# Holding the filter once in 32-row blocks and summing the complex product ahead of the inverse transform, in a fused FFT mixing and maxout kernel

## The chip, the cores and the metric

One core of a Trainium2 chip. The metric is the device time of one execution in microseconds, the median of the runs. Engines: TensorE (PE) multiplies matrices, VectorE (DVE), ScalarE (ACT) and GpSimd (POOL) work on elements, SyncE (SP) issues DMAs. [...]

## The reference

For x of 8 x 3072 x 256 (float32), a filter F = filt_r + i filt_i of 1537 x 256, and weights w1, w2 (256 x 1024) and w_out (1024 x 256):

```python
X = np.fft.rfft(x, axis=1)
Y = X * F
y = np.fft.irfft(Y, n=3072, axis=1)      # 24576 rows of 256 after a reshape
out = np.maximum(y @ w1, y @ w2) @ w_out
```

## The kernel before

**The maths.** 3072 = 96 x 32. S1 is a transform over 96 points, S2 one over 32 points with the twiddle factors (table `U`, 24 blocks u of 64 columns: 32 real, 32 imaginary parts), then comes the product with F, then S3, the inverse of S2 (tables `VP` for the part multiplied by filt_r, `VQ` for that by filt_i), and S4, the inverse over 96. From batch 2 on S1 works on sums and differences of the two halves of the input, which POOL makes (`fold`, lines 103 and 104) from float32 tiles `XF` that SP loads. Between the stages a batch goes through DRAM (`ad` between S1 and S2, `zd` between S3 and S4), which turns its axes. Maxout is computed as max(y(w1-w2), 0) w_out + y w2 w_out: `Wd` = w1-w2, `M` = w2 w_out, so each tile of 384 rows needs 8 pairs of `ph` matmuls (`moe_h`, line 454, then a relu on ACT or DVE) and 30 `po` matmuls (`moe_o`, lines 484 and 486).

**The filter.** `F` (line 51) has 128 partitions: for each of two groups g the rows 64g to 64g+31 hold the filter (16 rows of k, 16 of the mirrored 96-k), and rows 64g+32 to 64g+63 the same again, since S2 puts real parts in the first 32 rows and imaginary parts in the next 32. `load_f` loads one copy with 16 POOL DMAs, `double_f` makes the second: for h = 0 four DVE copies, for h = 1 four DMAs on SP. `put_fz` and `fix_f` put in the rows for k = 0, 48 and 1536.

**A visit.** The transforms of the next batches are threaded through the maxout of this one. The loop at line 709 runs 64 steps a batch: `moe_h` of one block, then a visit if one is planned for this step, then 3 or 4 `moe_o` matmuls, then the other planned work (`todo`: loads, folds, reads), then, once in 8 steps, `s4`. A visit n (line 415) does S3 of visit n-1 (line 405, 16 matmuls of 64x64 tiles), S2 of two of the 12 w (line 381, 8 matmuls), S1 of some quads of the next batch (line 354, 4 matmuls each) and the products of this S2 (line 387). A product is one DVE operation over 128 x 1024 that reads a PSUM tile `px` and writes px times filt_r and px times filt_i in bf16; S3 then adds real and imaginary parts in PSUM, by a second matmul with `VQ`. There are 7 visits to a batch, planned by hand in `plan_f2` (line 682), as are the loads (`xs`), the folds and the reads.

**PSUM.** The pool `ps` has six banks for everything but the outputs, which have two of their own (`pso`). A new tile takes the bank that was released first and waits until what was in it has been read.

**Order.** The program has `manual_schedule`: every engine and every DMA queue executes its instructions in the order of the program. What stands behind a waiting instruction waits too.

**The opening** handles batch 0 on its own path: `s1t`, transposes `t1`, S2, products shared by DVE and POOL (`products`, line 608; POOL's take a copy `xs` in SBUF that ACT makes, line 603), `s3t`, transposes `t2`, `s4`. The tables VP and VQ are made from U in `table_v` and `put_v`. POOL's queue there is: loads of x, loads of F, products, then the load of batch 1's quads 4 to 7 of 16 (line 645), Wo, Wd (lines 646 to 648), the rest of batch 1, and w2.

## Time and profile before

| | us |
|---|---|
| median of 3 runs | 501.41 (500.83 to 502.92) |
| span of the profiled execution, first to last instruction | 499.6 |
| median less that span | 1.8 |
| PE busy, span 62 to 490 | 427.65 of 428.00 |
| PE busy, span 0 to 36 | 27.15 of 36.00 |
| DVE, ACT, POOL busy over the span | 329.9, 309.0, 258.7 |

A line of the timeline reads: start and duration in us, engine, line of the kernel, operation, out<-in by the program's names, shape, count; in brackets how long the engine was idle ahead of it and what ended that. For PE the shape has the tile of the array (64*64) ahead of the operand's. A group of the profile reads: the same names, count | busy us, mean ns of one | idle time ahead and what ended it. The profiled execution has no time of its own beside its span; the runs were other executions.

### The profile page before, as it was taken

What the parts mean: (1) busy time and instruction counts of PE and PEld (TensorE: products, weight loads), DVE (VectorE), ACT (ScalarE), POOL (GpSimd) and SP (SyncE); (2) the same over time, 40 slices, a digit from 0 to 9 for tenths busy, and PEclk for the clock granted to TensorE, in tenths of its full rate; (3) what the DMA queues carried; (4) which work ended last, traced back from release to release, by engine and by line L of the source; (5) the groups of instructions that cost most, each with busy time, mean ns of one, the idle gap of its engine ahead of it and who ended that gap; (6) DMA issues with size and microseconds to landing.
All of it is one profiled execution on the core that took longest, in us unless ns stands there. A gap on an engine that the chain in (4) does not pass through costs nothing.

```text
span 499.6 us, 13073 instructions
## 1 busy us (share of the span) xinstructions
PE 486.2 (97%) x5297; PEld 361.0 (72%) x5300; DVE 329.9 (66%) x515; ACT 309.0 (62%) x630; POOL 258.7 (52%) x342
## 2 busy tenths in 40 slices
PE   7689999999999999999999999999999999999996
PEld 3457767777777777777777777777777777777775
DVE  7786788458865578457865678557774588555552
ACT  5777478647774577646775577646676456544442
POOL 8795569637546584539547394438642221222220
PEclk9989999999999999999999999999999999999999
DMA  8989799997689768896489776896677625521112
GB/s 130 159 236 219 216 245 298 277 258 210 206 241 245 206 202 219 257 261 195 150 252 251 197 231 189 261 261 181 199 205 206 158 85 149 172 83 64 64 64 85
DMA packets 78046, 97.23 MB, mean 195 GB/s; under 512 B 8065, under 2 KB 54434, under 8 KB 77954
## 3 DMA queue, kind: packets, MB, share of 16 engines
q1 hardware_dynamic: 64786, 66.80, 50.5%
q0 software_dynamic: 13200, 29.60, 20.7%
q8 instruction: 41, 0.67, 0.6%
q14 instruction: 19, 0.16, 0.1%
HBM read 53.87 MB, written 47.19 MB: 202 GB/s over the span
## 4 chain that ended last, share of the span: by engine, by line
PE 83%; DMA 11%; POOL 3%; SPq 1%; DVE 1%; issue 1%; ACT 0%; POOLq 0%
PE po L486 32%; PE ph L454 30%; PE po L484 8%; PE pz L405 4%; PE py L434 4%; DMA zd<-zt 2%; DMA bt<-ad 2%; DMA WS<-in_moe_w_dram 2%; PE px L381 2%; PE pa L354 2%; DMA xb<-in_x_dram 2%; POOL F L121 1%; DMA ad<-at 1%; POOL xb L88 1%; DMA F<-in_filt_i_dram 1%; DMA zr<-zd 1%
## 5 line engine op out<-in xcount | busy, mean ns | idle before, releaser
L486 PE MATMUL po<-Wo,gt 128*128 128x256 bf16 x1536 | 261.1, 273 | 0.0
L458 ACT ACTIVATE gt<-ph 128x384 bf16<-128x384 f32 x321 | 157.6, 495 | 146.8 <-PE ph L454 145.7
L486 PEld LDWEIGHTS <-gt 128*128 128x128 bf16 x1536 | 146.0, 98 | 66.7 <-issue 12.0
L467 POOL DMA_DIRECT2D out_dram<-ot x186 | 102.7, 557 | 170.8 <-DVE ot L499 166.4
L456 DVE TENSOR_SCALAR gt<-ph 128x384 bf16<-128x384 f32 x191 | 104.5, 553 | 64.3 <-PE ph L454 60.7
L387 DVE TENSOR_TENSOR pq<-px,F 128x1024 bf16<-128x1024 f32 x91 | 106.9, 1219 | 26.4 <-PE px L381 26.2
L454 PEld LDWEIGHTS <-Wd 128*128 128x128 bf16 x1024 | 96.5, 98 | 12.2 <-issue 0.3
L103 POOL TENSOR_TENSOR xb<-XF 128x512 bf16<-128x512 f32 x48 | 61.2, 1275 | 52.8 <-DMA XF<-in_x_dram 52.0
L499 DVE COPY ot<-po 128x512 f32<-128x512 f32 x95 | 65.2, 686 | 24.9 <-PE po L486 24.8
L104 POOL TENSOR_TENSOR xb<-XF 128x512 bf16<-128x512 f32 x48 | 60.9, 1269 | 0.0
L358 ACT ACTIVATE at<-pa 128x512 bf16<-128x512 f32 x96 | 51.8, 612 | 4.6 <-PE pa L354 4.6
L409 ACT ACTIVATE zt<-pz 128x512 bf16<-128x512 f32 x84 | 45.6, 595 | 4.9 <-PE pz L405 0.8
L434 PE MATMUL py<-G,zr 96*128 96x96 bf16 x512 | 32.6, 206 | 0.1
L434 PEld LDWEIGHTS <-zr 96*128 96x128 bf16 x512 | 28.9, 97 | 2.4 <-DVE zr L563 0.6
L405 PE MATMUL pz<-pq,VP 64*64 64x256 bf16 x336 | 22.0, 281 | 0.0
L381 PE MATMUL px<-bt,U 64*64 64x256 bf16 x384 | 20.2, 278 | 1.3 <-ACT VQ L278 0.7
L405 PE MATMUL pz<-pq,VQ 64*64 64x256 bf16 x336 | 21.0, 269 | 0.0
L405 PEld LDWEIGHTS <-VP 64*64 64x64 bf16 x336 | 9.9, 105 | 13.3 <-issue 13.0
L354 PE MATMUL pa<-xb,CT 64*64 64x512 bf16 x192 | 18.1, 377 | 0.3 <-DVE y__1495 L440 0.3
L381 PEld LDWEIGHTS <-U 64*64 64x64 bf16 x384 | 10.5, 108 | 4.2 <-issue 3.6
L570 PE MATMUL pd<-W 128*128 128x512 bf16 x28 | 10.1, 474 | 1.5 <-DVE zero L149 1.5
L405 PEld LDWEIGHTS <-VQ 64*64 64x64 bf16 x336 | 10.0, 106 | 0.0
(428 smaller groups left out, 602.9 us busy)
## 6 DMA issues: line engine op xcount, KB each, us to landing
out_dram<-ot POOLq DMA_DIRECT2D x186, 128.0 KB, 3.7
XF<-in_x_dram SPq DMA_DIRECT2D x96, 192.0 KB, 4.6
ad<-at SPq DMA_DIRECT2D x56, 192.0 KB, 3.7
zd<-zt SPq DMA_DIRECT2D x42, 256.0 KB, 3.1
zr<-zd SPq DMA_DIRECT2D x56, 192.0 KB, 4.6
bt<-ad SPq DMA_DIRECT2D x13, 768.0 KB, 10.5
WS<-in_moe_w_dram SPq DMA_DIRECT2D x4, 512.0 KB, 8.1
xb<-in_x_dram POOLq DMA_DIRECT2D x8, 192.0 KB, 6.6
```

Of the source, the lines that this page charges most:

```text
L103: G.tensor_tensor(t_[:, 0], f[:, 0], f[:, 1], OP.add)
L104: G.tensor_tensor(t_[:, 1], f[:, 0], f[:, 1], OP.subtract)
L358: S.activation(at[:, m0:m0 + 2], pa[g], AF.Copy)
L387: E.tensor_tensor(pq, px.rearrange("p (o i) d -> p o i d", o=1).to_broadcast([128, 2, 2, D]), F[:, :, 2 * v:2 * v + 2, s], OP.mult)
L405: TE.matmul(pz[g][64 * s:64 * s + 64, i], tab[64 * g:64 * g + 64, 2 * v + i, s], pq[s][64 * g:64 * g + 64, q, i], start=(q == 0), stop=(q ...
L434: TE.matmul(py[:, m], zr[b][:, 4 * i + m, 128 * dc:128 * dc + 128], G1, start=True, stop=True)
L454: TE.matmul(ph, Wd[:, dc, 128 * j:128 * j + 128], y_[:, dc], start=(dc == 0), stop=(dc == 1))
L456: V.tensor_scalar(gt[tt][:, j], ph, 0.0, None, OP.max)
L458: S.activation(gt[tt][:, j], ph, AF.Relu)
L467: E.dma_start(out=dst, in_=ot[tt // 2][:, 3 * (tt % 2) + c])
L486: TE.matmul(p_, g_[:, n - 2, blk], Wo[:, n - 2], start=(e == 0), stop=(e == 9))
L499: V.tensor_copy(ot[tt // 2][:, e - 1:e + 1], po[q // 2 % 2])
```

## The change

The filter is held once, in blocks of 32 rows: partition 32q + r of `F` holds, for 6 values of j, the row for block u = 4j + q, so that all 128 partitions differ. S2 writes the real parts and the imaginary parts of four blocks side by side, as two column groups c of one PSUM tile. This takes 64x32 tiles (16 matmuls for what 8 did), and so does S1 (8 for 4). A product now multiplies both c by both parts of the filter, in float32, and the complex sum is made ahead of S3: real parts by a subtraction on DVE, imaginary parts by an addition on POOL, each 128 x 512. S3 then needs no second pass over `VQ`: it works in 32x64 tiles on four blocks of 32 rows, once for two j, three times a batch, with 32 matmuls each and four PSUM banks. The visits at steps 11, 16, 21, 27, 32, 37 and 47 do S3 at the fourth, sixth and seventh, and S1 in pairs of quads at the others; folds and loads are planned anew. In the opening no filter rows are doubled, `load_f` has 20 DMAs, the loads of w1 and w2 are held until POOL has issued them (`hold_w`), S3 takes four terms into one sum (`TERMS`), and the load of batch 1's quads 4 to 7 stands behind Wd.

```diff
-    def s2(b, v):
+    def s2(b, j):
         px = [ps.tile([128, 2, D], FP32, tag="ps", name="px%d" % s) for s in range(2)]
+        for c in range(2):
+            for q, s in ((0, 0), (1, 1), (2, 0), (3, 1), (0, 1), (1, 0), (2, 1), (3, 0)):
+                u = 4 * j + q
+                TE.matmul(px[s][32 * q:32 * q + 32, c], U[64 * s:64 * s + 64, u, 32 * c:32 * c + 32],
+                          bt[b][64 * s:64 * s + 64, u], start=True, stop=True)
+        return px
...
+    def products(b, j, px):
+        pq = pqpool.tile([128, 2, 2, 2, D], FP32, tag="pq", name="pq")
+        for s in range(2):
+            product(V, j, s, px[s], pq[:, s])
+        zc[b, j] = zcpool.tile([128, 2, 2, D], BF16, tag="zc", name="zc")
+        V.tensor_tensor(zc[b, j][:, :, 0], pq[:, :, 0, 0], pq[:, :, 1, 1], OP.subtract)
+        G.tensor_tensor(zc[b, j][:, :, 1], pq[:, :, 0, 1], pq[:, :, 1, 0], OP.add)
+
+    def s3(b, t):
...
+        pz = [ps.tile([128, 2, D], FP32, tag="ps", name="pz%d" % q) for q in range(4)]
         for i in range(2):
+            z_ = zc.pop((b, 2 * t + i))
+            for c in range(2):
+                for q, s in ((0, 0), (1, 1), (2, 0), (3, 1), (0, 1), (1, 0), (2, 1), (3, 0)):
+                    TE.matmul(pz[q][64 * s:64 * s + 64, i], VT[32 * q:32 * q + 32, c, 2 * t + i, s],
+                              z_[32 * q:32 * q + 32, s, c], start=(c == 0), stop=(c == 1))
...
+    def visit(b, ts, js, quads):
+        for t in ts:
+            s3(b, t)
+        pxs_ = [s2(b, j) for j in js]
         if b + 1 < B:
             for c in quads:
                 s1(b + 1, c)
+        for j, px in zip(js, pxs_):
+            products(b, j, px)
...
-        for g, r in ((0, 0), (1, 1), (0, 1), (1, 0)):
-            TE.matmul(pa[g][64 * r:64 * r + 64], CT[64 * g:64 * g + 64, r], xb[b, c][64 * g:64 * g + 64, r],
-                      start=True, stop=True)
+        for h in range(2):
+            for g, s in ((0, 0), (1, 1), (0, 1), (1, 0)):
+                TE.matmul(pa[g][64 * s + 32 * h:64 * s + 32 * h + 32], CT[64 * g:64 * g + 64, s, h],
+                          xb[b, c][64 * g:64 * g + 64, s], start=True, stop=True)
...
+    hold_w()
+    for h in range(2):
+        load_w(h)
...
+    pz = s3t(0)
+    for q in range(4):
+        put_z(0, q, S, pz)
+    pxs[4] = s2(0, 4)
+    stage_x(4, 1)
+    dve(4, 0)
+    pool_(4, 1)
...
-    load_x(1, 2, 2)
     load_wo()
     for q in range(4):
         prep_wd(q, G)
+    load_x(1, 2, 2)
     for c in (4, 6):
         load_x(1, c, 2)
...
+            ts = {3: (0,), 5: (1,), 6: (2,)}.get(n, ())
+            js = (n,) if n < 6 else ()
+            mid.setdefault((b, st), []).append((visit, (b + 1, ts, js, quads[n])))
...
+    plan_f2(0, (23, 27, 31, 35, 38, 42, 48), ((0,), (1,), (2, 3), (), (4, 5), (), ()),
+            (8, 10, 15, 18, 21, 27, 30, 33), (16, 19, 25, 28, 31, 34, 38, 42), 57)
+    mid[0, 45] = [(visit, (1, (), (), (6,)))]
+    mid[0, 51] = [(visit, (1, (), (), (7,)))]
+    plan_f2(1, (11, 16, 21, 27, 32, 37, 47), ((0, 1), (2, 3), (4,), (), (5, 6), (), (7,)),
+            range(-25, 31, 7), range(-15, 41, 7), 52)
+    for b in range(2, B - 1):
+        plan_f2(b, (11, 16, 21, 27, 32, 37, 47), ((0, 1), (2, 3), (4, 5), (), (6, 7), (), ()),
+                range(-32, 24, 7), range(-21, 35, 7), 38)
```

## The prediction

> **What bounds the kernel now.** First the busy rows. TensorE (PE) is busy for 97% of the span, and nothing else comes above 72%. Windows of the trace split that: PE misses 0.35 us of the 428.0 from 62 to 490, so time is won or lost there only by PE's own slots or by making PE wait. Before 36 us it misses 8.85, and there other chains decide.

> ```profile
> PE 486.2 (97%) x5297; PEld 361.0 (72%) x5300; DVE 329.9 (66%) x515; ACT 309.0 (62%) x630; POOL 258.7 (52%) x342
> ```

> Then PE's timeline around one visit (start, duration, line; a row's duration has the drain in it, so I count from start to start):

> ```profile
> 230.77 0.49 PE L454 MATMUL ph<-y__4292,Wd 128*128 128x384 bf16 x2
> 231.19 0.30 PE L405 MATMUL pz<-pq,VP 64*64 64x256 bf16 x4
> 231.32 0.28 PE L405 MATMUL pz<-pq,VQ 64*64 64x256 bf16 x4
> 231.43 0.28 PE L405 MATMUL pz<-pq,VP 64*64 64x256 bf16 x4
> 231.54 0.28 PE L405 MATMUL pz<-pq,VQ 64*64 64x256 bf16 x4
> 231.65 0.39 PE L381 MATMUL px<-bt,U 64*64 64x256 bf16 x8
> 231.87 0.39 PE L354 MATMUL pa<-xb,CT 64*64 64x512 bf16 x4
> 232.19 0.39 PE L486 MATMUL po<-Wo,gt 128*128 128x256 bf16 x2
> ```

> Four 64x64 tiles run side by side, and a set of four with 256 columns costs 0.109 us. S3 of one visit is 0.46, S2 0.22, S1 0.21. Entering tiled work costs 0.09 (two ph matmuls take 0.33, the visit begins 0.42 after them), leaving it 0.1 (0.32 for S1). Almost every visit looks like this, so hardly any waits for a bank now.

> Third, the engines that PE would wait for:

> ```profile
> L387 DVE TENSOR_TENSOR pq<-px,F 128x1024 bf16<-128x1024 f32 x91 | 106.9, 1219 | 26.4 <-PE px L381 26.2
> L103 POOL TENSOR_TENSOR xb<-XF 128x512 bf16<-128x512 f32 x48 | 61.2, 1275 | 52.8 <-DMA XF<-in_x_dram 52.0
> L104 POOL TENSOR_TENSOR xb<-XF 128x512 bf16<-128x512 f32 x48 | 60.9, 1269 | 0.0
> ```

> Last, the opening: POOL's timeline, and the row of PE's that takes the second half of batch 1's input.

> ```profile
> 33.55 0.56 POOL L88 DMA_DIRECT2D xb<-in_x_dram  x1
> 34.10 0.93 POOL L293 DMA_DIRECT2D Wo<-in_moe_w_out_dram  x1
> 35.02 2.52 POOL L297 TENSOR_TENSOR Wd<-WS 128x512 bf16<-128x512 f32 x2
> 37.71 2.50 POOL L297 TENSOR_TENSOR Wd<-WS 128x512 bf16<-128x512 f32 x2 [0.17 <-DMA WS<-in_moe_w_dram]
> ```

> ```profile
> 40.97 0.38 PE L329 MATMUL pa<-xb,C 96*96 96x512 bf16 x1
> ```

> **The change, part by part.** The sum is made against the span, 499.6; the median of the runs is 501.4, 1.8 more, and that is added at the end.

> *S3.* A batch had 6 x 16 matmuls in fours; it has 3 x 32 in eights. No row shows 32x64 tiles. The best end is eight in the time of four: 3 x 0.46 instead of 6 x 0.46, -1.38 a batch, -9.7 over seven batches. The worst is no overlap beyond four, 0. The nearest rows are 64x32 tiles (lines 266 and 268): with 64 columns eight begin in about 0.033 us, against 0.031 for four 64x64 ones at line 264. That is overlap by eight, so I take -9.7.

> *S1 and S2* have twice the matmuls of half the width, by the same rows in the same time: 0. [...]

> *Tilings.* S3 and S2 no longer share one. Two visits of a batch change it midway, at an entry's 0.1: +0.2 a batch, with batch 1's extra stretch +1.6.

> *Banks.* PSUM pool `ps` has six, and every visit follows a ph. A ph's bank comes free 0.85 (ACT) or 0.92 us (DVE) after its second matmul begins, 0.60 to 0.67 into the visit, and some 0.05 later PE knows. A visit with S2 and two S1 quads takes six banks and wants the sixth at 0.22+0.21 = 0.43: a wait of 0.23. (Today's six-bank visits want it at 0.68 or later, so they don't wait.) There are 21 such visits; six hide it under the next item's wait: 15 x 0.23 = +3.4. S3 with S2 wants its sixth at 0.56: 14 x 0.13 = +1.8. Two stalls of today, 0.65 at 69 us and 0.37 at 113, go. Sum +4.2.

> *POOL's sum in front of the folds.* This is the dearest item. Today POOL has nothing of the products. After, each visit puts a 128x512 sum on POOL that waits for both of DVE's products, and POOL keeps its order, so a fold planned just behind a visit waits too. For batches 1 to 5 the last fold stands at step 27 or 28, right behind the visit at 27, and its S1 at step 32. From the first S3 matmul of visit 27: S2's second set begins at 0.46+0.1+0.11 with 0.13 for the bank, 0.80; DVE starts 0.32 after it (231.76 to 232.08); two products take 2.27 (232.08 to the next DVE start, 234.35): 3.4; POOL's sum, as line 103, 1.27: 4.7; the fold 2.5: 7.2. PE gets there by 0.46+0.1+0.22+0.1+0.13 for visit 27, 4.02 for five steps (0.33 a ph pair, 0.109 an output matmul, 0.34 for s4, 0.09 to enter) and 0.43 of S2 and the first S1: 5.5. It waits 1.7, five times: +8.5. In batch 0 the sums of steps 23 and 27 and the folds of 25 and 28 stand in one row on POOL; fold 3 ends 6.7 after visit 27 begins, S1 wants it at 4.3: +2.3. The other quads, worked out alike, have one us to spare or more. Sum +10.8.

> *DVE's subtraction* (128x512, two SBUF inputs) has no row of its size. Below it is 0.38 (line 233, 192 elements), above 0.96 (line 244, 768); between them 0.70 as a duration and, by the 0.1 that DVE's rows overlap, 0.6 from start to start. A visit then takes 2.87 of DVE instead of 2.27. A five-step stretch with its visit lasts 4.02+0.76 = 4.8; DVE's other work is 2.76 in eight steps (three relus and a y of 0.465, 1.5 copies of 0.60, from start to start), 1.7 in five, with 2.87 together 4.6. It fits, so 0, with nothing over.

> *Opening.* Four DVE copies (line 127, 4.76 us) and four SP DMAs go, and products begin with the first third of F. Today F lands from 14.8 (the last of x) to 25.5, a third by 18.4; DVE's t1 copies end by 19.1 as now, so products begin near 19.3 instead of 24.3. But ACT's queue then holds the chain: put_fz to 20.2 (0.93, as line 248), three t1 copies of 1.0, two tables of 0.87 and an xs of 0.6 to 25.5, when PSUM is free for s3t(0); its 128 matmuls at 0.0145 (line 539: two in 0.029) take 1.9 and ACT sees them 0.3 later, 27.7; four put_z copies of 0.55 stand ahead of the last xs (0.6), 30.5; POOL's last product (2.13) ends near 32.7 instead of 33.55. Then come Wo (0.93) and Wd (5.0), and only then, at 38.7, the load of batch 1's second quarter, which ran ahead of them at 33.55. Issue 0.56, then 3.7 (the median of an output block of 128 KB) to 6.7 us (the median of this row's size): it lands at 43.0 to 46, and PE stands at step 5 of tile 0 for it, which it passed at 40.97. Wo has landed by then and the queue is empty, so I take 43.2, near the lower end: +2.2. If POOL ends its products by 30.7, it is 0.

> *At nothing:* put_z's split, four S1 write DMAs for two (0.4 of SP's queue a piece, and S2 reads them steps later), and z_read in thirds (the first chunk is needed 12 us after the last S3; four copies of 0.55, a write and a read take near 11.5). Without that cover the z read costs about 0.5 a batch.

> Sum: -9.7 + 1.6 + 4.2 + 10.8 + 2.2 = +9.1; span 508.7, time **510.5**.

> **Rivals.** (1) *Faster: the folds are in time.* If sums pass POOL without holding a fold, the 10.8 goes (the six hidden bank waits, 1.4, come out), and with the x load in time the 2.2 too: 501.4 - 9.7 + 1.6 + 5.6 = 498.9, and 496.3 if the tiles then also start 2.6 earlier, as they could by POOL's end at 30.7 instead of 33.55 and a put_z that costs 0.25 more. For it: POOL is only 52% busy and DVE's wait for px is short. Against: the order on POOL is fixed, and the chain above has only row durations in it. It decides when the fold ends within 5.5 us of its visit. 0.22.

> (2) *Slower: eight row-and-column tiles don't overlap.* S3's second operand sits in four row groups, which no row shows. If it runs in fours, the 9.7 is not won: 520.2. 0.12.

> (3) *DVE becomes the bound.* The subtraction is the only DVE row with both inputs in SBUF in the steady part. In the opening four such adds (line 233) took 1.35 us beside a POOL cast and 1.16 without one. If a fold half (1.27) lies in the way, DVE's 4.6 of 4.8 overflows by up to 1.1; at one visit in eight of 42 it is +5.8: 516.3. 0.10. [...]

> (4) *No measurable change*: the waits come to about what S3 gives, 499 to 504. 0.10.

> My forecast, slower by PE's waits, 505 to 515, gets 0.46. A measurement here tells 0.5% (2.5 us) from no change. Faster 0.22 (rival 1), within 0.10 (rival 4), slower 0.68 (the rest). The range reaches down to rival 1 and up to rival 2: 495 to 521.

> **What would show each step.** S3: 32 matmuls in 0.46. Tilings: 0.1 between S3 and S2. Banks: a gap of 0.2 before the fourth set of a double visit. Folds: PE idle 1.7 us in the middle of the visit at step 32, ended by POOL's line of the fold. Opening: PE idle before the fifth f1, ended by an x DMA. If PE still misses under 1 us from 62 to 490, the forecast is wrong and rival 1 right.

## The result, and the profile after

The changed kernel takes 570.5 us (median of four runs, 568.9 to 572.2) against 501.8: 1.138 times as long (95% interval 1.134 to 1.142). The forecast was 510.5. Its profiled execution has a span of 567.1 against 499.6, and the mean granted clock of TensorE fell from 0.993 to 0.955. Times here and in the table are medians without executions more than 1.5% above the fastest of their kernel (three of four of e11, two of four of e15; the traces of these two are of such executions, so their lags are too long).

The busy row of the page after:

```profile
PE 507.5 (89%) x6014; PEld 359.2 (63%) x6014; DVE 366.5 (65%) x561; ACT 308.8 (54%) x631; POOL 323.2 (57%) x386
```

PE is no longer busy throughout, and nothing else is full either. Windows of the trace after (stretch, length, busy time of PE, PEld, DVE, ACT and POOL, granted clock, DMA share, GB/s):

```profile
62.00:490.00 428.00, 390.31 (x4509) 273.52 (x4507) 295.14 (x419) 238.41 (x487) 265.62 (x291) 0.97 0.67 188
0.00:36.00 36.00, 22.86 (x479) 13.35 (x479) 20.82 (x52) 20.63 (x40) 24.81 (x46) 0.86 0.80 149
```

From 62 to 490 PE now misses 37.7 us where it missed 0.35, and runs at 0.97 of its clock where it ran at 1.00. So most of the loss is waits. The busy time rose too, from 486.2 to 507.5, in part because of stretches at a lower clock (below).

To see where, I compared the start of every step's first `ph` matmul with the same step before. The lag is 10.8 us at the first step of batch 0, grows by 14.8 in batch 0, by 41.3 in batches 1 to 5 (7 to 9 in each), by 1.0 in batch 6, which has no S1, and by nothing in batch 7, which has no visits: 67.9 in all.

What the change was to win is there. PE's timeline around the visit at step 27 of batch 3:

```profile
285.30 0.49 PE L437 MATMUL ph<-y__4970,Wd 128*128 128x384 bf16 x2
285.72 0.64 PE L391 MATMUL pz<-zc,VT 32*64 32x256 bf16 x32
286.30 0.56 PE L361 MATMUL px<-bt,U 64*32 64x256 bf16 x16
286.78 0.28 PE L469 MATMUL po<-Wo,gt 128*128 128x256 bf16 x1
```

32 matmuls of S3 and the change to S2's tiles take 0.58 from start to start, where 16 took 0.46 before: eight 32x64 tiles do run side by side (a set of eight begins every 0.109, as a set of four 64x64 did before, and some 0.11 goes to the change). S2 then takes 0.48 where 0.32 (0.22 and the exit) was due, by a wait of 0.16 for a bank (its second set begins at 286.44, 0.05 after a DVE relu of 285.83 to 286.39).

The groups that answer to those of before, the two sums and S4's matmuls (line, engine, operation, count, busy us, mean ns, idle time ahead and what ended it):

```profile
L370 DVE TENSOR_TENSOR pq<-px,FP 128x1024 f32<-128x1024 f32 (+1 forms) x84 | 99.1, 1216 | 24.3 <-PE px L361 14.2
L381 POOL TENSOR_TENSOR zc<-pq 128x512 bf16<-128x512 f32 x42 | 63.6, 1514 | 54.5 <-DVE pq L370 41.2
...
L417 PE MATMUL py<-G,zr 96*128 96x96 bf16 x512 | 33.1, 208 | 12.2 <-DMA zr<-zd 11.8
L380 DVE TENSOR_TENSOR zc<-pq 128x512 bf16<-128x512 f32 x42 | 41.3, 982 | 1.4
```

Three things were not in the forecast: the subtraction takes 0.98 in the mean instead of 0.70, the addition 1.51 instead of 1.27, and PE waits 11.8 us for z.

**The opening.** POOL's timeline after:

```profile
20.11 1.04 POOL L116 DMA_DIRECT2D FP<-in_filt_i_dram  x2
26.91 1.04 POOL L116 DMA_DIRECT2D FP<-in_filt_i_dram  x2 [5.77 <-DMA FP<-in_filt_r_dram]
27.94 0.10 POOL L259 MEMSET WS<- 1x8 f32 x1
28.00 2.12 POOL L370 TENSOR_TENSOR pq<-xs,FP 128x1024 bf16<-128x1024 f32 x1
```

POOL issues the last loads of F 5.8 us late: the issue waits for the landing of a load issued eight loads earlier, at 16.75 (its 64 pieces of 4 KB as written took 9.9 us). In the trace's records the DMAs of POOL take eight semaphores in turn (numbers 99 to 106), and these issues wait for the last load on their own semaphore: the load of 16.75, landed at 26.63, and the issue of 26.91 both have number 101. So the eight may be a matter of the program's semaphores, and a limit of the queue is not shown. DVE stands for F even longer. The input of batch 1, which the forecast feared for, comes almost in time (below, the fifth f1, the S1 matmul of batch 1 in the opening, against 40.97 before; the step it stands at is 12.0 late after 10.8 at step 0):

```profile
30.16 2.35 DVE L370 TENSOR_TENSOR pq<-px,FP 128x1024 bf16<-128x1024 f32 x2 [8.21 <-DMA FP<-in_filt_i_dram]
```

```profile
53.00 0.38 PE L306 MATMUL pa<-xb,C 96*96 96x512 bf16 x1
```

**Half clock.** The windows around the wait for z at the end of batch 2:

```profile
250.00:253.00 3.00, 3.00 (x26) 2.31 (x24) 1.33 (x3) 1.42 (x3) 1.28 (x3) 1.00 1.05 343
253.00:256.40 3.40, 0.28 (x3) 0.00 (x0) 0.44 (x1) 0.00 (x0) 3.24 (x4) 1.00 0.36 112
256.40:259.80 3.40, 2.82 (x17) 1.91 (x18) 0.56 (x1) 0.98 (x2) 0.30 (x1) 0.50 0.92 287
259.80:263.00 3.20, 3.20 (x27) 2.49 (x26) 1.71 (x3) 1.17 (x3) 1.80 (x2) 1.00 0.90 241
```

At the end of this wait of 3.7 us (to 256.98) the granted clock falls to 0.50, for 3.41 us from 256.41. In all, the trace has 0.50 in six stretches from 62 to 490 us, where the trace before has none (1.00): 10.24 us from 82.33, at the waits of batch 0 (2.04 to 82.44, 2.27 to 86.56), and five of 3.41. PE is busy for 23.1 of these 27.3 us, so they cost at most 11.5 us (an estimate: half of the busy time, as if all of it ran twice as fast at the full clock). The length of the wait alone does not decide it. Half clock follows waits of 2.04 us (to 125.97) and 2.85 us (to 388.82), and in batches 4 and 5 two waits of 0.73 and 0.85 at step 32 (the stretches begin at 358.81 and 427.08). It does not follow the same two waits in batches 2 and 3 (to 226.89 and 293.70), nor the wait of 3.18 us that ends at 322.91:

```profile
318.00:323.00 5.00, 1.82 (x16) 1.20 (x15) 1.21 (x2) 0.79 (x2) 4.41 (x6) 1.00 0.67 214
323.00:327.00 4.00, 4.00 (x37) 3.10 (x37) 1.94 (x4) 1.96 (x4) 0.00 (x0) 1.00 0.95 281
```

All six stretches last 3.41 us or three times that. What starts one is not shown.

### The profile page after: what moved, and what is told of

The parts are those of the page before. It is cut to its first block, busy times and chain, and to the rows that moved or that the text cites. A ratio compares the mean times of both kernels' runs of the same rounds, so it can differ in the third digit from the quotient of the medians.

```text
span 567.1 us, 14690 instructions
## 1 busy us (share of the span) xinstructions
PE 507.5 (89%) x6014; PEld 359.2 (63%) x6014; DVE 366.5 (65%) x561; ACT 308.8 (54%) x631; POOL 323.2 (57%) x386
## 4 chain that ended last, share of the span: by engine, by line
PE 53%; DMA 17%; DVE 8%; POOL 5%; issue 4%; SPq 3%; ACT 2%; POOLq 0%; DVEq 0%
PE po L469 19%; PE ph L437 19%; DMA XF<-in_x_dram 7%; DMA zd<-zt 6%; PE po L467 5%; DVE pq L370 5%; PE py L417 3%; POOL xb L104 2%; DMA bt<-ad 2%; POOL xb L103 2%; PE pz L391 2%; DMA zr<-zd 2%; PE pa L332 2%; PE px L361 1%; SPq L95 1%
## 5 line engine op out<-in xcount | busy, mean ns | idle before, releaser
L469 PE MATMUL po<-Wo,gt 128*128 128x256 bf16 x1536 | 266.0, 277 | 2.4 <-DVE gt L439 2.4
L370 DVE TENSOR_TENSOR pq<-px,FP 128x1024 f32<-128x1024 f32 (+1 forms) x84 | 99.1, 1216 | 24.3 <-PE px L361 14.2
L437 PEld LDWEIGHTS <-Wd 128*128 128x128 bf16 x1024 | 98.7, 100 | 16.4 <-issue 2.8
L381 POOL TENSOR_TENSOR zc<-pq 128x512 bf16<-128x512 f32 x42 | 63.6, 1514 | 54.5 <-DVE pq L370 41.2
L103 POOL TENSOR_TENSOR xb<-XF 128x512 bf16<-128x512 f32 x48 | 61.5, 1280 | 47.7 <-DMA XF<-in_x_dram 44.3
L104 POOL TENSOR_TENSOR xb<-XF 128x512 bf16<-128x512 f32 x48 | 61.4, 1278 | 0.0
L395 ACT ACTIVATE zt<-pz 128x512 bf16<-128x512 f32 x84 | 43.4, 602 | 10.5 <-PE pz L391 9.9
L417 PE MATMUL py<-G,zr 96*128 96x96 bf16 x512 | 33.1, 208 | 12.2 <-DMA zr<-zd 11.8
L380 DVE TENSOR_TENSOR zc<-pq 128x512 bf16<-128x512 f32 x42 | 41.3, 982 | 1.4
L332 PE MATMUL pa<-xb,CT 64*32 64x512 bf16 x384 | 24.8, 391 | 18.6 <-POOL xb L103 7.8
L417 PEld LDWEIGHTS <-zr 96*128 96x128 bf16 x512 | 29.1, 99 | 15.2 <-DMA zr<-zd 10.6
L332 PEld LDWEIGHTS <-CT 64*32 64x32 bf16 x384 | 7.7, 90 | 31.4 <-issue 16.2
L361 PE MATMUL px<-bt,U 64*32 64x256 bf16 x768 | 21.6, 280 | 4.8 <-DVE gt L439 2.9
L361 PEld LDWEIGHTS <-U 64*32 64x32 bf16 x768 | 8.2, 90 | 17.9 <-issue 17.1
L522 PE MATMUL pt<-VT,pq 32*128 32x64 bf16 x384 | 6.7, 233 | 11.8 <-POOL VT L252 7.2
L391 PE MATMUL pz<-zc,VT 32*64 32x256 bf16 x672 | 15.1, 274 | 0.3 <-ACT gt L441 0.2
```

The source lines that it names most:

```text
L103: G.tensor_tensor(t_[:, 0], f[:, 0], f[:, 1], OP.add)
L104: G.tensor_tensor(t_[:, 1], f[:, 0], f[:, 1], OP.subtract)
L370: E.tensor_tensor(pq, px.rearrange("p (o c) d -> p o c d", o=1).to_broadcast([128, 2, 2, D]), F[:, :, j, s].rearrange("p r (o d) -> p r o ...
L381: G.tensor_tensor(zc[b, j][:, :, 1], pq[:, :, 0, 1], pq[:, :, 1, 0], OP.add)
L417: TE.matmul(py[:, m], zr[b][:, 4 * i + m, 128 * dc:128 * dc + 128], G1, start=True, stop=True)
L437: TE.matmul(ph, Wd[:, dc, 128 * j:128 * j + 128], y_[:, dc], start=(dc == 0), stop=(dc == 1))
```

## The experiments

Theory at first: separate waits in four places (F's loads, folds behind POOL's sum, the read of z, DVE late behind a visit), each to be taken away by its own edit. Rivals: DVE's load sets everything, or the DMA engines do. The times, with the lag against the kernel before, by the traces, at step 0 and then grown in batch 0, in batches 1 to 5, and in batch 6:

| | median us | ratio, 95% interval | step 0 | batch 0 | 1 to 5 | 6 |
|---|---|---|---|---|---|---|
| changed kernel | 570.5 | 1.134 to 1.142 | 10.8 | 14.8 | 41.3 | 1.0 |
| e1_f_order | 568.4 | 1.127 to 1.142 | 7.6 | 13.9 | 45.7 | 1.0 |
| e2_folds | 562.8 | 1.116 to 1.128 | 9.3 | 13.6 | 36.7 | 1.0 |
| e3_z_earlier | 566.8 | 1.121 to 1.135 | 10.7 | 14.4 | 40.1 | 1.0 |
| e4_pq_bf16 | 560.8 | 1.109 to 1.129 | 9.9 | 11.2 | 36.8 | -0.1 |
| e5_no_add | 555.6 | 1.107 to 1.110 | 10.5 | 14.0 | 31.5 | 0.9 |
| e6_four | 553.7 | 1.100 to 1.111 | 8.9 | 12.8 | 31.6 | -0.1 |
| e7_xf_gap | 564.6 | 1.123 to 1.131 | 10.0 | 11.6 | 42.3 | 1.0 |
| e8_no_sums | 543.9 | 1.082 to 1.093 | 10.6 | 10.4 | 20.9 | -0.4 |
| e9_read_late | 556.1 | 1.100 to 1.115 | 10.3 | 15.5 | 24.3 | 1.0 |
| e10_relus | 562.6 | 1.112 to 1.126 | 10.7 | 14.0 | 40.1 | -0.3 |
| e11_waits_out | 540.3 (one run) | none | 9.4 | 15.9 | 22.6 | -0.1 |
| e12_waits_out_relus | 542.0 | 1.070 to 1.088 | 13.5 | 9.0 | 24.4 | -0.4 |
| e13_no_f_rest | 567.1 | 1.124 to 1.137 | 6.4 | 13.2 | 44.8 | 1.0 |
| e14_plan_of_before | 562.4 | 1.114 to 1.128 | 10.1 | 14.2 | 39.7 | 0.6 |
| e15_plan_bf16 | 547.0 (two runs) | 1.085 to 1.096 | 8.1 | 12.3 | 33.0 | -0.1 |
| e16_plan_bf16_relus | 538.4 | 1.066 to 1.078 | 9.0 | 7.9 | 22.0 | -0.7 |
| e17_both_on_pool | 546.0 | 1.087 to 1.092 | 9.2 | 12.9 | 22.3 | -0.8 |
| e18_both_on_pool_all | 538.6 | 1.071 to 1.084 | 9.5 | 10.8 | 17.1 | -0.9 |

**e1_f_order**

```diff
+    load_fn(0, 2)
+    load_fn(2, 6)
     for j0, j1 in ((0, 2), (2, 6)):
         load_f(j0, j1)
```

`load_fn` holds the two loads of whole rows, taken out of `load_f`, which keeps the reversed ones.

> The loads of F that take one long piece from each of 64 partitions are all issued first, ahead of the sixteen reversed ones; nothing else differs from the changed kernel (570.5). Theory (POOL's DMA queue holds eight transfers, and the ninth waits for the landing of the first): the waits of 5.8 and 1.8 us on POOL at 21.2 and 14.0 go, POOL's first product starts by 24 instead of 28.0, tile 0 starts some 4 us earlier, 566. Rival (the transfer itself sets it, 3.1 MB read): the last piece of F lands near 30 in any order, POOL's first product stays at 27 to 28, 570.

POOL's wait of 5.77 went, its first product started at 24.25, tile 0 3.2 us earlier (45.8). The time did not follow by an amount that can be told (2.1 less, and the intervals overlap): the lag grew by as much again in batches 1 to 5. Waits move.

**e2_folds**

```diff
-    plan_f2(0, (23, 27, 31, 35, 38, 42, 48), ((0,), (1,), (2, 3), (), (4, 5), (), ()),
+    plan_f2(0, (23, 27, 31, 35, 38, 42, 48), ((0,), (1,), (), (2,), (3,), (4,), ()),
...
-                range(-32, 24, 7), range(-21, 35, 7), 38)
+                range(-34, 22, 7), range(-23, 33, 7), 38)
```

> Loads and folds for the visit at step 32 two steps earlier in batches 1 to 5 (ahead of the sum of visit 27); in batch 0, S1 of quads 2 and 3 at steps 35 and 38 instead of 31, quads 4, 5 at 42 and 45. Theory (PE waits for folds that stand on POOL behind a sum or behind their loads): the 1.9 us at step 32 go five times, the 6.9 us of batch 0 too, and the 5 us that its half clock costs afterwards: 549 to 554. Rival (DVE is late anyway, and the S1 that no longer waits for a fold waits for a bank): 565 or more.

Between the two. The fold waits went, but in batch 0 PE now waits at steps 38 and 42 for DVE (3.8 and 3.1 us), and z is later (4.4 to 4.8). The subtraction's mean rose to 1.20.

**e3_z_earlier and e7_xf_gap** look for what makes z late: its own chain, or the x loads around it.

```diff
...
-    plan_f2(1, (11, 16, 21, 27, 32, 37, 47), ((0, 1), (2, 3), (4,), (), (5, 6), (), (7,)),
+    plan_f2(1, (11, 16, 21, 27, 32, 37, 44), ((0, 1), (2, 3), (4,), (), (5, 6), (), (7,)),
...
```

> The last S3 of a batch at step 44 instead of 47 (in batch 0 at 45 instead of 48, its S1 of quad 6 changes places with it), and the read of its z with it. Theory (the chain copy, write, read of z is too long for the 12 us it has): the waits before the first py of batches 1, 3, 4 and 5 (2.2, 3.9, 3.3 and 3.0 us) go, with some half-clock time behind them: 555 to 558. Rival (the DMA engines are full, and z lands when they have worked off the rest): PE still waits 2 us or more at three of the four places, 566 or more.

```diff
-                range(-32, 24, 7), range(-21, 35, 7), 38)
+                (-32, -25, -12, -8, -4, 3, 10, 17), range(-21, 35, 7), 38)
```

> The loads of x that stood at steps 39, 46 and 53 of a batch, around the last write and read of z, are put at 52, 56 and 60, so that SP's queue and the DMA engines have no load of x between steps 40 and 51; nothing else differs. Theory (the last z of a batch is late since its write stands behind x loads in the queue and on the DMA engines): the waits of 2.2 to 3.9 us before the first py go, 12.4 in all, 556 to 560. Rival (the chain of four copies, write and read is too long by itself): 2 us or more stay at three of the four places, 566 or more.

Both miss: about 2 us of each wait stay at the ends of batches 2 to 4 (1.8 to 2.4 in e3, 2.1 to 2.5 in e7). Neither the length of the chain nor the x loads is the cause by itself. SP's timeline of the changed kernel shows what else is there:

```profile
301.09 0.38 SPq L396 DMA_DIRECT2D zd<-zt  x1
301.58 1.92 SPq L347 DMA_DIRECT2D bt<-ad  x2
303.56 4.13 SPq L95 DMA_DIRECT2D XF<-in_x_dram  x2
307.73 1.83 SPq L354 DMA_DIRECT2D zr<-zd  x4
309.66 3.92 SPq L95 DMA_DIRECT2D XF<-in_x_dram  x2
314.26 0.38 SPq L396 DMA_DIRECT2D zd<-zt  x1
320.34 1.71 SPq L354 DMA_DIRECT2D zr<-zd  x4
```

The input of the next S2 (`bt`, 768 KB a piece) is read at 301.58, in the middle of the batch; the x loads behind it hold SP some 4 us for two; the last z is written at 314.26, though its copies end at 309.9, and landed only by 320.3. What stands ahead of the write is the second of the two x loads. It waits in its turn for a piece of `bt` (SP's waits from 300 to 325: total us, times, longest):

```profile
SPq L95 <- DMA bt<-ad: 3.2, 1, 3.2
```

SP's DMAs, too, take eight semaphores in turn in the trace's records (108, 109, 111, 112 and 114 to 117), and this load, issued at 313.25, has that of the `bt` piece issued at 302.26 and landed at 313.23, number 109. In e7, with no x load there, the write goes out at 309.54 but lands 9.0 us later. PE waits for z:

```profile
322.91 0.51 PE L417 MATMUL py<-G,zr 96*128 96x96 bf16 x8 [3.18 <-DMA zr<-zd]
```

**e9_read_late** moves that read. (Its expectation says that it stood at step 58 before; the plan of before has it at 53.)

```diff
-                range(-32, 24, 7), range(-21, 35, 7), 38)
+                range(-32, 24, 7), range(-21, 35, 7), 52)
```

> One number changes: from batch 2 on, the read of the next batch's S2 input (768 KB twice, planned at step 38 in the changed kernel, 58 in the kernel before) stands at step 52, behind the last read of z. Theory (this read fills the DMA engines and SP's queue for some 9 us ahead of the last write of z, which is why z is late in batches 2 to 4 and not in batch 1, where the read is at 52 already): the 3.9, 3.3 and 3.0 us before the first py go, 558 to 561. Rival (the loads of x around it, or the 512 KB write itself): 2 us or more stay at two of the three, 567 or more.

All three waits went: 14.4 us for one number, the dearest single item of the plan among those tried. The shorter wait for z at the end of batch 0 is another one: of its 2.2 us, e9 keeps 1.6, and there the read stood at 52 or later all along. SP's timeline of e9, same place:

```profile
305.22 0.38 SPq L396 DMA_DIRECT2D zd<-zt  x1
308.87 1.72 SPq L354 DMA_DIRECT2D zr<-zd  x4
310.64 1.82 SPq L347 DMA_DIRECT2D bt<-ad  x2
```

The write goes out as soon as the copies are done and lands in 3.7 us instead of 6.1.

**e4_pq_bf16**

```diff
-        pq = pqpool.tile([128, 2, 2, 2, D], FP32, tag="pq", name="pq")
+        pq = pqpool.tile([128, 2, 2, 2, D], BF16, tag="pq", name="pq")
```

> The two products of a visit are written in bf16 instead of float32, so both sums read half the bytes. Theory (DVE is late after a visit because its subtraction takes 0.98 us instead of the 0.7 it has when POOL is idle): the subtraction falls to 0.7 or less, the waits that DVE ends at steps 21 and 26 (about 11 us) go for the most part, 560 to 565. Rival (the two engines exclude each other for a whole instruction, however many bytes it reads): the subtraction's mean stays above 0.9 and the time within 2 us of 570.5.

The time fell by 9.7, as expected. The subtraction's mean fell from 0.98 to 0.77 only, not to 0.7 or less, and of the waits that DVE ends at step 21 about half stayed. And the spread did not fit the theory: 0.43 at the least and 3.2 at the most.

**e5_no_add and e8_no_sums**

```diff
-        G.tensor_tensor(zc[b, j][:, :, 1], pq[:, :, 0, 1], pq[:, :, 1, 0], OP.add)
...
-                              z_[32 * q:32 * q + 32, s, c], start=(c == 0), stop=(c == 1))
+                              (z_ if c == 0 else ZI)[32 * q:32 * q + 32, s, c], start=(c == 0), stop=(c == 1))
```

> POOL's sum is left out (the imaginary part of the filtered spectrum is read from a tile of zeros instead, so the result lacks it); the rest is the changed kernel. Theory (POOL's sum costs twice, by holding folds and by slowing DVE's subtraction beside it): subtraction back at about 0.7, the 9.4 us at step 32 of batches 1 to 5 and most of the 11 us that PE waits for DVE go: 550 to 556. Rival (the load on DVE by itself, 42 subtractions and four-input products, is what makes DVE late): DVE's waits at steps 21 and 26 stay, 560 or more.

> Both sums are left out, DVE's and POOL's: S3 reads one of the two products instead of the sum, from a bf16 tile (so the result lacks the other term); the rest is the changed kernel. Theory (the sums ahead of S3 are what the steady part loses by): the waits for folds at step 32 and for DVE at steps 21 and 26 go, 9.4 and 11 us, and some of batch 0's: 542 to 550, and the rest of the loss is the opening (11) and the z reads (12). Rival (DMA transfers set the steady part, and the sums only show where they do not): 558 or more.

(The edit above is that of e5.) Without the addition the fold waits at step 32 went in all five batches, though in batch 3 PE waits 1.6 us there for DVE in their place. But the subtraction kept its mean (1.01): the folds lie in its way too. Without both sums, the waits for DVE at steps 21 and 26 and for those folds went, 26.6 us, which rules out the rival of e8, that DMA sets the steady part (558 or more). e8 also writes the products in bf16, in four buffers, as S3 reads them directly; each still takes 1.21, as before. What stayed in e8: the opening, 10.4 in batch 0, and z. In batch 0 the fold still comes 5.6 us too late though POOL has no sum to make; its timeline and SP's in e8:

```profile
81.01 1.26 POOL L103 TENSOR_TENSOR xb<-XF 128x512 bf16<-128x512 f32 x1 [4.14 <-DMA ad<-at]
```

```profile
68.88 1.55 SPq L320 DMA_DIRECT2D bt<-ad  x3
70.48 2.08 SPq L95 DMA_DIRECT2D XF<-in_x_dram  x1
```

POOL had been idle for 4.1 us. Its input was planned at step 15 and issued behind the read of `bt`, which waits for the landing of `ad`. So batch 0's wait looks like one for a load; the bracket names `ad`, which a fold does not read, and no run moves this load, so this is read from the two timelines only.

**e6_four** (e1's order, e2's batch 0 and folds, e4, e7's gap), **e10_relus**, **e11_waits_out** (e1's order, e2's batch 0 with quads 4, 5 and 6, 7 paired, the last folds earlier, e4, e9, and in the opening the sign change and one product from POOL to DVE) and **e12_waits_out_relus** (both). e10's edit:

```diff
-        if (tt, j) in on_v if tt < 8 else j in (1, 3, 6):
+        st, late = 8 * (tt % 8) + j, (23, 27, 31, 35, 38, 42) if tt < 8 else (11, 16, 21, 27, 32, 37)
+        on_dve = (tt, j) in on_v if tt < 8 else j in (1, 3, 6)
+        if on_dve and (tt > 55 or not any(v < st < v + 4 for v in late)):
```

> Four edits at once: the order of F's loads of e1, products in bf16 of e4, the gap in the x loads of e7, S1 of batch 0 later as in e2 and the last folds of a batch two steps earlier. If the waits are separate costs, their gains add up: 2, 8 and 10 us as measured for e1, e2 and e4, and some 10 for the gap, about 540. If each wait that goes uncovers another one behind it, because DVE is late at all of them, less than two thirds of that comes, 550 or more.

> Relus that DVE did in the three steps behind a visit (8 of 24 a batch, six in batch 0) go to ACT; nothing else differs from the changed kernel. Theory (DVE is late behind a visit, and holds PSUM banks by its late relus): the waits that a DVE relu ends at steps 21 and 26, about 11 us, go, and the sum of POOL starts earlier, so some of the fold waits too: 556 to 562. Rival (ACT is late there as well, with the copies of S1, and takes its place): within 3 us of 570.5.

> The edits that went after one wait each, together, each in its better form: F's loads as in e1, the two sign changes of the table and one product moved from POOL to DVE in the opening; S1 of batch 0 at later visits; the last three folds of a batch one to two steps earlier with their loads; the S2 read at 52; products in bf16. If the waits stand side by side, the gains add: about 570.5 - 2 - 4 (opening) - 8 (folds) - 10 (bf16) - 11 (read) = 535. If DVE is late under all of them, 548 or more.

> As the last one, with the relus of e10 on ACT as well. If DVE's lateness is what the other edits run into, this gives more here than alone: 10 us or more under the last one, 515 to 530. If ACT takes its place, no more than 3 us.

In e6 the gains did not add: it won 16.8 of the 30 that its parts promised. e11 won 30.2 of its 35, by a single run. Relus alone won 7.9, just short of the theory's range (562.6, where 562 was its upper end), and on top of e11 nothing that can be told (542.0 against 540.3), as the rival of e12 had it. The moves in the opening won nothing that the traces show (in e12 tile 0 starts at 51.6, against 45.8 in e1). Something under all of these was left.

**e13_no_f_rest**

```diff
-    for j0, j1 in ((0, 2), (2, 6)):
-        load_f(j0, j1)
+    load_f(0, 2)
+    G.memset(F[:, :, 2:6], 0.5)
```

> The second part of the load of F is left out; those rows of the filter are set to a constant by POOL instead (so the result lacks the filter there). The rest is the changed kernel. Theory (the opening is late because the last of F lands at 28 to 30 instead of 24): POOL's second product starts by 26, tile 0 starts by 43 instead of 49.0. Rival (POOL's queue, with two sign changes of 1.2 us each and four products, or the copies on ACT set it anyway): tile 0 starts at 46 or later.

Between the two: tile 0 starts at 44.5. The late part of F explains at least 4.4 us of the opening's 10.8 (10.8 less 6.4). It may be more, since e13's own memset costs something: beside it and the POOL product behind it a bf16 copy on DVE (line 130) takes 4.75 us instead of 0.21, and the product queued behind it 4.04 instead of 1.22. The order behind F explains the rest (POOL's last product ends at 35.1 instead of 39.3, then come the last S3, copies, transposes, and the four f1 that now stand behind s4, with a further 2.2 us wait ahead of them that the trace does not name).

**e14_plan_of_before, e15_plan_bf16, e16_plan_bf16_relus**

```diff
...
+    for b in range(1, B - 1):
+        plan_f2(b, (14, 18, 23, 31, 34 if b < B - 2 else 35, 39, 47), ((0,), (1,), (2,), (3,), (4,), (5,), (6, 7)),
+                range(-25, 31, 7), range(-14, 42, 7) if b > 1 else range(-15, 41, 7), 53)
...
```

> The changed stages in the plan of the kernel before: visits, S1 (one quad a visit, two at the last), loads, folds and the reads stand at the steps where they stood. Theory (what the steady part loses lies in the plan: S1 in pairs ahead of its folds, the read of S2's input ahead of z, pairs that want six banks): the waits for folds and z go and only DVE's remain: 530 to 540, of which the opening is 11. Rival (the sums themselves: a visit is too long for DVE and POOL in any plan): 548 or more.

> The plan of before, and two more edits: products in bf16, and the order of F's loads of e1. If what is left in e14 is the length of the sums and the opening's queue, this is 6 to 12 us below e14; if neither is on the path there, within 3 us of it.

> As e15, and the relus in the three steps behind a visit that makes products go from DVE to ACT. If DVE's lateness behind a visit is the last thing that PE waits for there, some 5 us under e15; if ACT is as late, within 2 us of it or above. For this to be faster than the kernel before, the opening's 8 us would have to be won back too, which no edit here does: over 505.

e15 is 15.4 below e14 (6 to 12 were expected) and e16 8.6 below e15 (some 5), so both are on the path. e14 decides for its rival. In the plan of before the waits for z and for folds are gone, and the time is 562.4 all the same: the sums lose it in this plan too. Here that is seen best. DVE, POOL and PE of e14 around step 23 of batch 3:

```profile
269.13 2.36 DVE L370 TENSOR_TENSOR pq<-px,FP 128x1024 f32<-128x1024 f32 x2
271.52 5.03 DVE L380 TENSOR_TENSOR zc<-pq 128x512 bf16<-128x512 f32 x1
```

```profile
271.16 1.12 POOL L450 DMA_DIRECT2D out_dram<-ot  x2
272.29 1.28 POOL L381 TENSOR_TENSOR zc<-pq 128x512 bf16<-128x512 f32 x1
273.52 1.27 POOL L103 TENSOR_TENSOR xb<-XF 128x512 bf16<-128x512 f32 x1
274.74 1.26 POOL L104 TENSOR_TENSOR xb<-XF 128x512 bf16<-128x512 f32 x1
275.96 1.71 POOL L381 TENSOR_TENSOR zc<-pq 128x512 bf16<-128x512 f32 x1
```

```profile
277.68 1.09 PE L332 MATMUL pa<-xb,CT 64*32 64x512 bf16 x8 [3.98 <-POOL zc L381]
```

A subtraction that takes 0.69 us alone takes 5.03 here. When it starts, POOL is issuing two DMAs; 0.77 later POOL's sum begins, then the two halves of a fold. The subtraction ends at 276.55, after the last of these (276.0), and the next POOL sum, begun at 275.96, takes 1.71 instead of 1.26. So the subtraction did not get in while POOL went from one operation to the next, and ended 0.55 after the last of them; why it did not get in ahead of the sum of 272.29 is not shown. PE waits 4 us: its weights wait for a relu that stands behind the subtraction on DVE (277.08 to 277.6), while the line names POOL's sum, which ended at the same moment.

That the subtraction and POOL's operations on tensors excluded each other for whole operations is seen over the ten runs with float32 sums: 252 subtractions began with POOL idle, and none took over 0.75; of 101 that began during an operation of POOL on a tensor, 96 did; of 67 that began while POOL issued a DMA, 17 did. In the changed kernel it is the same, milder (operation, count, min/median/max in ns):

```profile
L380 DVE TENSOR_TENSOR zc<-pq x42: 691/692/2761, 75.4 to 491.9; 128x512 bf16<-128x512 f32 x42
L381 POOL TENSOR_TENSOR zc<-pq x42: 1258/1674/1777, 75.4 to 492.1; 128x512 bf16<-128x512 f32 x42
```

34 of 42 subtractions take 0.69; the other eight began during an operation of POOL and take 1.25 to 2.76, six of them 2.4 and more, and each ends 0.55 to 0.56 after the end of an operation of POOL on a tensor. 24 of the additions start beside a subtraction and take 1.67 to 1.78, 0.4 more than alone. The products (one input from PSUM) and the relus keep their times in the steady part of every run, 1.20 to 1.23 and 0.54 to 0.56.

**e17_both_on_pool and e18_both_on_pool_all**

```diff
-        V.tensor_tensor(zc[b, j][:, :, 0], pq[:, :, 0, 0], pq[:, :, 1, 1], OP.subtract)
+        G.tensor_tensor(zc[b, j][:, :, 0], pq[:, :, 0, 0], pq[:, :, 1, 1], OP.subtract)
```

> e14 (the plan of before, 562.4) with the subtraction moved from DVE to POOL, beside the addition; nothing else. In e14 the subtraction takes 0.69 us where POOL's sums and folds leave it alone and up to 5.03 us where they run back to back (mean 1.42, so 31 us over 42). Theory (the two engines exclude each other on operands in SBUF for whole instructions, and POOL's row of instructions keeps DVE out): on POOL the two sums cost 1.27 each, DVE is never held, its waits at steps 18, 23 and 38 go: 530 to 542, although POOL has 53 us more to do. Rival (a visit holds more work than DVE and POOL have time for, whoever does it): POOL's folds are later by one sum a visit, and the time stays over 555.

(The "lock" of the next text is the exclusion that this one names.)

> As e17, with products in bf16 in four buffers instead of two, the order of F's loads of e1, and the relus behind a visit on ACT as in e16 (538.4). Theory of the lock: DVE has what it had in the kernel before, and what stays is the opening (8 to 9 us), some half clock behind it, and waits of S1 for banks (2 a batch): 518 to 528. Rival (what e16 still loses is not the lock): within 5 us of 538.

e17: 16.4 us less than e14 with 38 us more work on POOL, short of the range but far from the rival. e17 takes the subtractions themselves off DVE as well (29 us by 0.69 each) beside the 31 us of holding, and no run tells the two apart. The sums in e17:

```profile
L380 POOL TENSOR_TENSOR zc<-pq x42: 1253/1265/1285, 74.9 to 469.3; 128x512 bf16<-128x512 f32 x42
```

No sum is held any more; of PE's waits for DVE behind a visit one is left (0.7 at step 26 of batch 1). In their place PE waits for the sums themselves at the S3 of steps 35 to 46 of batch 0 and of step 39 of batches 1, 2 and 4, 1 to 3.4 us each. That is POOL's own load. e18 comes out level with e16 (538.6 and 538.4), not at 518 to 528, so its rival came true by the number. The traces show different waits under it: e16 waits for DVE (1.2 to 1.8 at step 23), e18 for POOL's sums (0.8 to 3.9 ahead of an S3). What e16 still lost by the exclusion, e18 loses by a later POOL, as far as the traces tell; no run has neither. No version beat the kernel before.

## Why the prediction was wrong, point by point

The sign was right, the size was 60 us short. Three terms of the sum failed. The first is "DVE's subtraction ... It fits, so 0, with nothing over": held by POOL it cost about 17 us (26.6 for both sums by e8, less 9.4 for folds). Rival (3) named this cause, and gave it 0.10 and 5.8 us. The second is the read of z, "At nothing", which cost 14 to 17 us (e9). The third is the opening, +2.2, which measured 10.8 to 11.8. Half clock behind some waits is in all of these and was in no term.

- *S3, -9.7.* Right: 0.47, and 0.11 for the change of tiling. *Tilings*: right by the same row.
- *Banks, +4.2.* The wait ahead of the second S1 of a pair is 0.28 to 0.29, not 0.23, and S3 with S2 waits 0.16 (0.48 less 0.32), not 0.13. In e8, batch 3 without its 4.4 us for z and behind it is 0.5 longer than before; the terms gave -0.25. So S3's gain is all eaten by banks and entries; over seven batches the forecast's -3.9 is about +3 (an estimate from this one batch).
- *POOL's sum ahead of folds, +10.8.* For batches 1 to 5 right in mechanism and size: PE waits 1.9 at step 32, not 1.7, five times 9.4. POOL and PE there:

```profile
289.52 1.68 POOL L381 TENSOR_TENSOR zc<-pq 128x512 bf16<-128x512 f32 x1 [0.88 <-DVE pq L370]
291.15 1.27 POOL L103 TENSOR_TENSOR xb<-XF 128x512 bf16<-128x512 f32 x1
292.38 1.26 POOL L104 TENSOR_TENSOR xb<-XF 128x512 bf16<-128x512 f32 x1
```

```profile
291.35 0.40 PE L332 MATMUL pa<-xb,CT 64*32 64x512 bf16 x8
292.48 0.37 PE L332 MATMUL pa<-xb,CT 64*32 64x512 bf16 x1 [0.73 <-POOL xb L103]
```

  The visit begins at 285.72; the sum starts 3.8 later (3.4 by the forecast) and the fold ends 7.9 later (7.2). For batch 0 the reason was wrong: 6.9 us instead of 2.3, by the load of x (read from e8), and behind it at most 3.3 us of half clock (half of PE's 6.6 busy in 10.24).
- *DVE's subtraction, 0.* The duration alone was right (0.69 for 0.70), but that it fits behind the products was not. Held by POOL it costs DVE 12.3 us more in the changed kernel (41.3 less 42 times 0.69) and POOL 10.7 (63.6 less 42 times 1.26); both sums together cost 26.6 (e8), of which folds 9.4. The row of rival (3), 1.35 against 1.16, was misread: it adds up four adds, of which only one was longer beside POOL. One by one, seven of the eight adds take 0.35. The eighth, and the cast beside it, in the kernel before:

```profile
7.89 0.55 DVE L233 TENSOR_TENSOR ua<-t,t 128x192 f32<-128x192 f32 x1
```

```profile
7.62 0.61 POOL L141 CAST F<-XF 32x256 bf16<-32x256 f32 x1
```

  The add begins inside the cast (which ends at 8.23), takes 0.20 more than the other seven, and ends 0.21 after the cast: as the subtractions of the runs do, it seems to have been held until POOL's operation ended. So one row of the trace before had it already, though not what a POOL that never pauses makes of it: 0.69 alone and up to 5.03 behind POOL's row in e14. I took the row's sum without reading it add by add.
- *At nothing: "put_z's split, four S1 write DMAs for two, and z_read in thirds".* The read of z was named with 0.5 a batch if uncovered; PE waited 2.2 to 3.9 us for it in four batches. For three of them (3.0 to 3.9) the reason is the read of S2's input, moved from step 53 to 38 (e9): a 1.5 MB transfer ahead of the last z on the same queue. It was in the diff and had no term at all.
- *Opening, +2.2.* 10.8 at step 0, and only 1.2 for the x load it was meant for. The landing of F was taken from before (25.5, here 29.8) with loads of another shape and number: at least 4.4 by e13.
- *Nothing was set down for what a wait does to the clock.* The trace has 27.3 us at half clock from 62 to 490, at most 11.5 us of loss, which is part of the amounts above.

The account closes roughly: opening 11.8 (lag at step 16), z 16.8 (lag of e9 against the change), sums 26.4 (lag of e8), batch 0's loads with their half clock some 9 (the 10.4 of e8 in batch 0 less what is counted with the opening, and with a z wait of 1.7 in it), S3 with banks some 3: 67 of 67.9. The parts come from different runs with one trace each, runs of one kernel lie up to 7 us apart (e9), and as e6 shows the parts are not independent; the split is exact to a few us only. What stays open is the 2.2 us ahead of the f1 in e13, and how much of e16's remaining 22 us in batches 1 to 5 is still the exclusion.

## What to carry to other kernels

Before an operation with two SBUF inputs is put on DVE, look at what POOL does at that time. Here the subtraction took 0.69 us with POOL idle and up to 5.03 behind POOL operations in a row (e14), and the relu queued behind it on DVE came late with it: PE waited 3.98 for weights that stood for this relu. A row that adds up several operations is read one by one before it decides a term. In a kernel like this, whose PE was 97% busy, every moved transfer needs a term of its own, by queue and by bytes, a read of 1.5 MB first of all (14.4 us in e9). Gains from waits that go need not add, since one wait can cover others (16.8 of some 30 us in e6); and some waits of the changed kernel were followed by 3.41 us or more at a clock of 0.50, at most 11.5 us of loss in all (the estimate above).
